# First batch's FFN input layer by halves of the tokens, with its taps in the product's PSUM bank

## The chip, the cores and the metric

One core of a Trainium2 chip. The metric is the device time of one execution in microseconds (us). The kernel before takes 770.74 us (median of 3 runs, 770.47 to 771.9).

## The reference

Three layers follow one another on 4 batches of 576 tokens. Arrays are float32.

```python
scores = scale * q @ k^T                            # 4 x 8 heads x 576 x 576, head width 64
scores = where(scores >= max(scores) - tau, scores, -1e9)
attn   = softmax(scores) @ v                        # heads side by side: x, 4 x 576 x 512
h  = relu(x^T @ w_tok1) @ w_tok2                    # token mixing, 576 -> 256 -> 576
u  = x + h^T
u  = u + relu(u @ w_ch1) @ w_ch2                    # channel mixing, 512 -> 1536 -> 512
h  = relu(u @ w_in)                                 # FFN input layer, 512 -> 1024
c  = w0 * h[s-1] + w1 * h[s] + w2 * h[s+1]          # three taps along the tokens, zero at both ends
out = (h * sigmoid(c)) @ w_out                      # FFN output layer, 1024 -> 512
```

## The kernel before, in words

**Tiling.** A batch has four pairs of heads. Attention works in chunks of 128 queries by 576 keys, nine for a pair, so 36 for a batch. A chunk's chain is: scores into two PSUM banks (`scores`), the row maximum on DVE (`exps`, tile `nm`), the threshold `thr`, the exponential on ACT (tile `e`), the mask on DVE (`mask`, L602), the float16 high half on ACT (`ph`, L607), the low half on POOL (`rest`, L611), one DMA transpose (L616), and the product with V (`pv`, L626 and L629) once the transpose has landed. In the first batch all of a chunk's tiles lie in a ring of four within the buffer `act_t`, so its transposes show as `act_t<-act_t`; later ones as `pt<-ph`. After a pair's nine chunks come the token mixing products (`tok`, L666, L681, L686), which give the transposed activations `u`, high and low half.

**Dense part** (`dense`). Channel mixing takes 12 tiles of w_ch1 (L793) and then 12 of w_ch2 (L811). The FFN input layer follows with 8 tiles `f` of 128 features (L844), and the output layer with five groups of 128 tokens `j` (L867, L870). Each product is three float16 passes. In the FFN input layer a tile's 576 tokens are computed as 256 and 320 columns, each in a PSUM bank that `dbank` hands out and `flush` takes back after the eviction. `h_out` evicts each part with a relu into the float32 tile `h` (L820), which frees the bank. After the second part `gate` works on all 576 tokens in a float32 SBUF tile `ct`: the first tap on ACT (L827), two more on DVE (L829), a tanh on ACT (L831), the product with `h` on DVE (L832), the high half on ACT (L833) and the low half on POOL (L834).

```python
A.activation(out=ct, in_=ht[:, 0:S], func=AF.Copy, scale=cw[:, 0, f:f + 1])
for kk in (1, 2):
    V.scalar_tensor_tensor(out=ct, in0=ht[:, kk:kk + S], scalar=cw[:, kk, f:f + 1], in1=ct, ...)
```

**Interleaving.** The dense part of batch b runs beside the attention of batch b+1: both are generators, advanced in proportion. The weights are loaded and split into halves while the first batch runs (`wload`, `float32`, called by `wstep`), through bank 4, which joins the free banks when the last weight has been asked for. Until then the first batch's dense part has banks 5 and 6.

**Order.** The instructions are first written down in that program order. The class `Order` then puts each engine's instructions in the order in which a list scheduler with fixed costs (`cost`, `send`) would start them, the earliest in program order first among those that are ready. For loads from DRAM there is a further rule, the `heels`: a load that is written down after the fourth and up to the 36th transpose may be placed only when the transpose four places back has been placed. SP issues almost all DMAs in that one order, so an issue that waits holds up those behind it. The 36th transpose is the last of the first batch.

```python
elif self.dma[x] and not self.area(i.ins[0])[9] and self.BEHIND < len(turned) <= self.FIRST:
    self.heels.setdefault(turned[-1 - self.BEHIND], []).append(x)
```

## Time and profile before

| | |
|---|---|
| median of 3 runs | 770.74 us |
| the profiled execution: its time, its span | 770.83 us, 769.0 us |
| busy share: PE, DVE, ACT, POOL | 95%, 66%, 59%, 54% |
| PE idle within the span | 42.2 us (769.0 less 726.8) |
| mean granted TensorE clock | 0.989 |
| chain that ended last: PE, DVE, DMA, POOL, ACT | 67%, 9%, 8%, 5%, 5% |

The share of a busy engine is a mean over stages. Attention of the first batch alone fills the first 97 us; channel mixing of batch 0 beside attention of batch 1 lasts to 226 us; the FFN of batch 0 follows to 300 us. Each further batch takes about 165 us, the last without attention beside it. In the rows below, a line number is that of the kernel before. A row of a group gives its busy time and mean duration, then the idle time of its engine ahead of it and whose end closed that idle time. In a timeline row the idle time ahead stands in brackets with its releaser.

### The profile page before, as it was taken

How to read it: one execution, taken by the hardware profiler on the slowest of the kernel's cores; microseconds unless marked ns; L12 is line 12 of the kernel's file. 1: busy time of each engine (PE TensorE's matmuls, PEld its weight loads, DVE VectorE, ACT ScalarE, POOL GpSimd, SP SyncE). 2: the span in 40 equal slices, each digit the busy share in tenths (PEclk: the TensorE clock that was granted, in tenths of full speed). 3: DMA queues.
4: the chain of work that ended last, by engine and by line, in shares of the span. 5: the costliest groups of instructions: out<-in, count | busy, mean ns of one | idle time of the engine just before them, and what ended most of it. 6: DMA issues, size and time to landing. Idle time of an engine off the chain costs nothing.

```text
span 769.0 us, 18598 instructions
## 1 busy us (share of the span) xinstructions
PE 726.8 (95%) x7398; PEld 543.3 (71%) x7398; DVE 511.2 (66%) x914; ACT 452.8 (59%) x927; POOL 417.8 (54%) x463
## 2 busy tenths in 40 slices
PE   7889769999998879999999999999999999999998
PEld 4567557777776646788888766778888766788764
DVE  6989768887789961676867952776866941323470
ACT  6977757776768842575657752665656842211471
POOL 5877689887878960466555840366464830000040
PEclk9999979999999999999999999999999999999999
DMA  8999999999997702579777502588863400000001
GB/s 215 224 182 177 265 228 211 240 213 229 204 237 170 156 15 83 122 134 158 159 140 135 86 15 93 114 148 148 153 118 63 78 29 35 1 1 2 1 1 62
DMA packets 200951, 97.00 MB, mean 126 GB/s; under 512 B 174752, under 2 KB 186784, under 8 KB 200864
## 3 DMA queue, kind: packets, MB, share of 16 engines
q1 hardware_dynamic: 200544, 95.55, 59.8%
q8 instruction: 58, 0.95, 0.5%
q10 hardware_dynamic: 320, 0.26, 0.1%
q14 instruction: 29, 0.24, 0.1%
HBM read 39.35 MB, written 4.72 MB: 57 GB/s over the span
## 4 chain that ended last, share of the span: by engine, by line
PE 67%; DVE 9%; DMA 8%; POOL 5%; ACT 5%; issue 4%; SPq 2%; ACTq 0%; POOLq 0%; DVEq 0%
PE ps L811 17%; PE ps L793 15%; PE ps L867 11%; PE ps L844 7%; PE ps L571 4%; PE ps L626 3%; DMA act_t<-act_t 3%; DVE ct L829 3%; PE ps L666 2%; PE ps L681 2%; PE ps L567 2%; PE ps L629 2%; DMA ld<-in_v_dram 1%; POOL ph L611 1%; DVE nm L583 1%
## 5 line engine op out<-in xcount | busy, mean ns | idle before, releaser
L611 POOL TENSOR_TENSOR ph<-e,ph 128x576 f16<-128x576 f32 x108 | 141.6, 1311 | 105.7 <-ACT ph L607 93.5
L811 PE MATMUL ps<-act_t,wc_h 128*128 128x256 f16 (+1 forms) x768 | 149.9, 286 | 0.0
L583 DVE TENSOR_REDUCE nm<-ps 128x1 f32<-128x576 f32 x144 | 107.6, 748 | 20.0 <-PE ps L571 12.8
L602 DVE SCALAR_TENSOR_TENSOR e<-ps,thr,e 128x576 f32<-128x576 f32 x108 | 87.6, 812 | 49.4 <-ACT e L595 41.4
L834 POOL TENSOR_TENSOR act_t<-ct,act_t 128x576 f16<-128x576 f32 x32 | 46.0, 1438 | 132.2 <-ACT act_t L833 130.8
L793 PE MATMUL ps<-u_h,wc_h 128*128 128x320 f16 (+1 forms) x384 | 109.6, 286 | 0.5 <-DVE u_l L689 0.5
L811 PE MATMUL ps<-act_t,wc_l 128*128 128x256 f16 (+1 forms) x384 | 109.7, 286 | 0.0
L793 PE MATMUL ps<-u_h,wc_l 128*128 128x320 f16 (+1 forms) x384 | 109.5, 286 | 0.0
L793 PE MATMUL ps<-u_l,wc_h 128*128 128x320 f16 (+1 forms) x384 | 109.1, 286 | 0.0
L793 PEld LDWEIGHTS <-wc_h 128*128 128x128 f16 x768 | 75.1, 98 | 21.5 <-issue 2.1
L811 PEld LDWEIGHTS <-wc_h 128*128 128x128 f16 x768 | 75.1, 98 | 21.0 <-issue 2.0
L867 PE MATMUL ps<-wo_h,act_t 128*128 128x512 f16 x256 | 77.3, 383 | 4.2 <-ACT h L820 4.2
L829 DVE SCALAR_TENSOR_TENSOR ct<-h,cw,ct 128x576 f32<-128x576 f32 x64 | 71.8, 1125 | 7.5 <-ACT ct L827 7.2
L844 PE MATMUL ps<-u_h,wi_h 128*128 128x256 f16 (+1 forms) x256 | 73.0, 286 | 3.5 <-ACT h L820 1.9
L607 ACT ACTIVATE ph<-e 128x576 f16<-128x576 f32 x108 | 73.1, 677 | 1.2 <-DVE e L602 0.8
L844 PE MATMUL ps<-u_h,wi_l 128*128 128x256 f16 (+1 forms) x256 | 73.1, 286 | 0.0
L844 PE MATMUL ps<-u_l,wi_h 128*128 128x256 f16 (+1 forms) x256 | 73.1, 286 | 0.0
L768 DVE SCALAR_TENSOR_TENSOR act_t<-ps,act_t 128x256 f16<-128x256 f32 x96 | 43.5, 455 | 43.2 <-ACT act_t L767 42.6
L867 PEld LDWEIGHTS <-act_t 128*128 128x128 f16 x384 | 36.9, 98 | 47.2 <-issue 6.4
L626 PE MATMUL ps<-vh,pt 128*128 128x65 f16 (+1 forms) x1080 | 68.8, 195 | 0.6 <-DVE x L646 0.6
L626 PEld LDWEIGHTS <-pt 128*128 128x128 f16 (+1 forms) x1080 | 61.2, 101 | 8.8 <-issue 5.7
L767 ACT ACTIVATE act_t<-ps 128x256 f16<-128x256 f32 x96 | 39.1, 407 | 47.9 <-PE ps L793 47.1
(123 smaller groups left out, 1670.5 us busy)
## 6 DMA issues: line engine op xcount, KB each, us to landing
st<-in_moe_w_ch_dram SPq DMA_DIRECT2D x24, 512.0 KB, 4.6
ld<-in_v_dram SPq DMA_DIRECT2D x32, 160.0 KB, 3.1
kt<-ks SPq DMA_DIRECT2D x32, 144.0 KB, 2.8
st<-in_moe_w_in_dram SPq DMA_DIRECT2D x8, 512.0 KB, 5.0
st<-in_moe_w_out_dram SPq DMA_DIRECT2D x8, 512.0 KB, 4.4
out_dram<-ot SPq DMA_DIRECT2D x16, 256.0 KB, 2.0
kt<-in_k_dram SPq DMA_DIRECT2D x16, 144.0 KB, 4.1
ld<-in_q_dram SPq DMA_DIRECT2D x8, 288.0 KB, 3.6
```

The lines of the kernel that those rows point to most:

```text
L583: V.tensor_reduce(out=nm, in_=c["s3"], axis=AX.XY, op=ALU.max, negate=True)
L602: V.scalar_tensor_tensor(out=e3, in0=c["s3"], scalar=c["thr"], in1=e3, op0=ALU.is_ge, op1=ALU.mult)
L607: A.activation(out=c["ph"][:, 0:S], in_=c["e"], func=AF.Copy)
L611: G.tensor_tensor(out=c["ph"][:, S:], in0=c["e"], in1=c["ph"][:, 0:S], op=ALU.subtract)
L626: T.matmul(dst[o:o + m], pt[:, j, o:o + m], vh[:, hh, j, 0:D + 1], start=(j == 0), stop=(j == NSL - 1))
L768: V.scalar_tensor_tensor(out=r_t(f, 1)[:, sl], in0=t, scalar=0.0, in1=r_t(f, 0)[:, sl], op0=ALU.max, op1=ALU.subtract)
L793: T.matmul(t, wc1[wx][:, f, c], u[c][ux][:, sl], start=(c == 0 and i == 0), stop=(c == NC - 1 and i == 2))
L811: T.matmul(t, wc2[wx][:, c, f], r_t(f, rx)[:, sl], start=(by_dve(c) and f == 0 and i == 0), stop=(f == NF - 1 and i == 2))
L829: V.scalar_tensor_tensor(out=ct, in0=ht[:, kk:kk + S], scalar=cw[:, kk, f:f + 1], in1=ct, op0=ALU.mult, op1=ALU.add)
L834: G.tensor_tensor(out=g_t(f, 1), in0=ct, in1=g_t(f, 0), op=ALU.subtract)
L844: T.matmul(t, wi[wx][:, f, c], u[c][ux][:, s0:s0 + n], start=(c == 0 and i == 0), stop=(c == NC - 1 and i == 2))
L867: T.matmul(t, g_t(f, gx)[:, j * P:(j + 1) * P], wo[wx][:, f], **lim)
```

## The change

Three edits. **First**, in the first batch the FFN input layer goes by halves of the tokens: all 8 tiles for the first half, then all 8 for the second. A half has 290 columns, the 288 tokens and one neighbour on each side (at the ends of the sequence the column is the zero margin or falls on the far side). `h_half` does the relu into one of four half-size slots in the two `h` tiles, writes the first tap back over the product in its PSUM bank, adds the two other taps there, applies the tanh there, and writes the product with `h` to an SBUF tile `ct`; only then is the bank free. `wstep` is called with 1 at each of the 16 halves instead of 2 at each of the 8 tiles. Batches 1 to 3 keep the form of before. **Second**, the `heels` rule: loads that are written down after the 31st to 36th transpose wait for the 36th to be placed. **Third**, in batches 0 and 1 (72 chunks) `thr` moves from DVE to ACT.

```diff
--- before.py
+++ after.py
@@ -33,12 +33,14 @@
         self.dma = [i.opcode in ("DMACopy", "DmaTransposeAnt") for i in self.ins]
         self.before, self.first, self.uses, self.turns = [set() for _ in range(n)], [[] for _ in range(n)], [[] for _ in range(n)], {}
         self.depend()
-        self.heels, turned = {}, []
+        self.heels, turned = {}, 0
+        turns = [x for x, i in enumerate(self.ins) if i.opcode == "DmaTransposeAnt"]
         for x, i in enumerate(self.ins):
             if i.opcode == "DmaTransposeAnt":
-                turned.append(x)
-            elif self.dma[x] and not self.area(i.ins[0])[9] and self.BEHIND < len(turned) <= self.FIRST:
-                self.heels.setdefault(turned[-1 - self.BEHIND], []).append(x)
+                turned += 1
+            elif self.dma[x] and not self.area(i.ins[0])[9] and self.BEHIND < turned <= self.FIRST:
+                heel = turned - 1 - self.BEHIND if turned <= self.LAST else self.FIRST - 1
+                self.heels.setdefault(turns[heel], []).append(x)
         self.after = [[] for _ in range(n)]
         for x in range(n):
             for y in self.before[x]:
@@ -143,7 +145,7 @@
         size = o[7] * o[8] * o[6]
         return size / (390 if size > 2e5 else 300), 500, 1450, 1250 if s[9] and o[9] else 1750 if o[9] else 1300
 
-    BEHIND, FIRST = 3, 36
+    BEHIND, LAST, FIRST = 3, 30, 36
     LAP = {"DVE": 85, "Activation": 103, "Pool": 44}
     LAG = {"DVE": 24, "Activation": 24, "Pool": 76, "SP": 17, "PE": 30}
 
@@ -437,10 +439,11 @@
 
     u_t = [[[const.tile([P, S], F16, name=f"u{i}_{c}_{x}") for x in "hl"] for c in range(NC)]
            for i in range(2)]
-    h_t = [const.tile([P, S + 2], F32, name=f"h{i}") for i in range(2)]
+    HW = S // 2 + 4
+    h_t = [const.tile([P, 2 * HW], F32, name=f"h{i}") for i in range(2)]
     for t in h_t:
-        V.memset(t[:, 0:1], 0.0)
-        V.memset(t[:, S + 1:S + 2], 0.0)
+        for o in (0, HW - 1, HW, 2 * HW - 1):
+            V.memset(t[:, o:o + 1], 0.0)
     v_t = [(const.tile([P, 2, 2 * NS + 1, D + 2], F16, name=f"vh{i}"),
             const.tile([P, 2, NS + 1, D], F16, name=f"vl{i}")) for i in range(2)]
     qk_t = [(const.tile([P, 2, S], F16, name=f"qt{i}"),
@@ -590,7 +593,7 @@
         if kind:
             G.tensor_scalar(out=thr, in0=nm, scalar1=-1.0, scalar2=mtaus[:, 1:2], op0=ALU.mult, op1=ALU.add)
         else:
-            V.tensor_scalar(out=thr, in0=nm, scalar1=-1.0, scalar2=mtaus[:, 0:1], op0=ALU.mult, op1=ALU.add)
+            A.activation(out=thr, in_=nm, func=AF.Identity, scale=-1.0, bias=mtaus[:, 0:1])
         e = half(i, 0).bitcast(F32) if i < PER else qk2.tile([P, S], F32, tag="x", name="e", bufs=15)
         A.activation(out=e.rearrange("p (a b) -> p a b", a=2), in_=c["s3"], func=AF.Exp, bias=bias,
                                    scale=sc)
@@ -833,9 +836,40 @@
             A.activation(out=g_t(f, 0), in_=ct, func=AF.Copy)
             G.tensor_tensor(out=g_t(f, 1), in0=ct, in1=g_t(f, 0), op=ALU.subtract)
 
-        for f in range(NG):
-            if b == 0:
-                wstep(2)
+        def h_half(f, x, t):
+
+            ht = h_t[f % 2][:, (f // 2 + x) % 2 * HW:][:, :HW]
+            A.activation(out=ht[:, 1:HW - 1], in_=t, func=AF.Relu, scale=1.0 / WS2)
+            ct = t[:, :hn]
+            A.activation(out=ct, in_=ht[:, 2 * x:2 * x + hn], func=AF.Copy, scale=cw[:, 0, f:f + 1])
+            for kk in (1, 2):
+                V.scalar_tensor_tensor(out=ct, in0=ht[:, 2 * x + kk:2 * x + kk + hn], scalar=cw[:, kk, f:f + 1], in1=ct,
+                                       op0=ALU.mult, op1=ALU.add)
+            A.activation(out=ct, in_=ct, func=AF.Tanh, scale=0.5 / SX)
+            gt = qk2.tile([P, S], F32, tag="x", name="ct", bufs=15)[:, :hn]
+            V.scalar_tensor_tensor(out=gt, in0=ct, scalar=1.0, in1=ht[:, 2 * x + 1:2 * x + 1 + hn], op0=ALU.add, op1=ALU.mult)
+            gh, gl = [g_t(f, y)[:, x * hn:(x + 1) * hn] for y in range(2)]
+            A.activation(out=gh, in_=gt, func=AF.Copy)
+            G.tensor_tensor(out=gl, in0=gt, in1=gh, op=ALU.subtract)
+
+        if b == 0:
+            for x in range(2):
+                for f in range(NG):
+                    wstep(1)
+                    bk = dbank()
+                    s0 = x * (hn - 2)
+                    t = ps[:, bk, :hn + 2]
+                    for c in range(NC):
+                        for i, (wx, ux) in enumerate(PASS):
+                            T.matmul(t, wi[wx][:, f, c], u[c][ux][:, s0:s0 + hn + 2],
+                                     start=(c == 0 and i == 0), stop=(c == NC - 1 and i == 2))
+                    flush()
+                    late.append((bk, lambda f=f, x=x, t=t: h_half(f, x, t)))
+                    yield
+            flush()
+            for t in h_t:
+                V.memset(t[:, S + 1:S + 2], 0.0)
+        for f in range(NG if b else 0):
             for s0, n in SPL:
                 bk = dbank()
                 t = ps[:, bk, :n]
```

How the order moves. On SP, around the last ten transposes of the first batch. Before (`st` are weights, `ld` is V, `qt` and `kt` are Q and K of the next batch):

```order
L347 DMA st<-in_moe_w_ch_dram 128x1024 x3
L616 DMA_TRANSPOSE act_t<-act_t 128x9x128 x4
L347 DMA st<-in_moe_w_ch_dram 128x1024
L513 DMA ld<-in_v_dram 128x320 x2
L616 DMA_TRANSPOSE act_t<-act_t 128x9x128 x4
L347 DMA st<-in_moe_w_ch_dram 128x1024
L473 DMA qt_166<-in_q_dram 128x576
L482 DMA kt_0_167<-in_q_dram 64x576
L616 DMA_TRANSPOSE act_t<-act_t 128x9x128
L528 DMA vh_159<-vh_159 64x2x264
```

And now, the same place:

```order
L349 DMA st<-in_moe_w_ch_dram 128x1024 x3
L619 DMA_TRANSPOSE act_t<-act_t 128x9x128 x9
L349 DMA st<-in_moe_w_ch_dram 128x1024
L516 DMA ld<-in_v_dram 128x320 x2
L349 DMA st<-in_moe_w_ch_dram 128x1024
L476 DMA qt_170<-in_q_dram 128x576
L485 DMA kt_0_171<-in_q_dram 64x576
L486 DMA kt_1_172<-in_k_dram 64x2x288
```

Six loads that stood among the last nine transposes now stand behind them.

On DVE, in the FFN input layer of the first batch. Before (L829 are the taps, L832 the product, L593 is `thr`, L583 the maximum, L602 the mask):

```order
L593 TENSOR_SCALAR thr<-nm,mtaus 128x1
L829 SCALAR_TENSOR_TENSOR ct<-h_154,cw,ct 128x576
L583 TENSOR_REDUCE nm<-ps 128x1
L829 SCALAR_TENSOR_TENSOR ct<-h_154,cw,ct 128x576
L593 TENSOR_SCALAR thr<-nm,mtaus 128x1
L602 SCALAR_TENSOR_TENSOR e<-ps,thr,e 128x576 x2
L832 SCALAR_TENSOR_TENSOR ct<-ct,h_154 128x576
```

And now (L846 are the taps, L850 the product, L388 and L390 convert weights, L586 and L605 are the maximum and the mask):

```order
L586 TENSOR_REDUCE nm<-ps 128x1
L846 SCALAR_TENSOR_TENSOR ps<-h_154,cw,ps 128x288 x2
L388 SCALAR_TENSOR_TENSOR ps<-st,ps 128x512
L850 SCALAR_TENSOR_TENSOR ct<-ps,h_154 128x288
L390 SCALAR_TENSOR_TENSOR wf<-st,ps 128x512
L605 SCALAR_TENSOR_TENSOR e<-ps,thr,e 128x576
L846 SCALAR_TENSOR_TENSOR ps<-h_153,cw,ps 128x288 x2
L586 TENSOR_REDUCE nm<-ps 128x1
```

Three instructions of 576 columns with SBUF operands have become six of 288 columns, each with one operand in PSUM; `thr` is gone.

On ACT, in the same stage, now (L842 is the relu, L844 the first tap, L848 the tanh, L852 the high half, L596 `thr`; L598, L610, L375 and L387 are the exponential, the chunk's high half and two steps of a weight):

```order
L848 ACTIVATE ps<-ps 128x288
L842 ACTIVATE h_154<-ps 128x290
L375 ACTIVATE wo_h<-wf 128x512
L852 ACTIVATE act_t<-ct 128x288
L844 ACTIVATE ps<-h_154,cw 128x288
L596 ACTIVATE thr<-nm,mtaus 128x1
L387 ACTIVATE ps<-st 128x512
L842 ACTIVATE h_153<-ps 128x290
L848 ACTIVATE ps<-ps 128x288
L598 ACTIVATE e<-ps,nm 128x576
```

The steps of two halves alternate, one in bank 5 and one in bank 6, with attention and weights between them. In the built program all 16 halves lie in these two banks in turn, a token mixing product of 30 matmuls takes bank 6 once between two halves, and bank 4 is first used behind the twelfth half, for a token mixing product and then for the output layer. On PE 16 matmuls of the output layer stand between the last four halves; after the last half come 14 matmuls of the output layer, 7 of `pv`, 18 of the output layer, 30 of token mixing and then the other 96 of the output layer. Before, all the output layer's matmuls stood behind the last tile of the input layer: 48, with 12 token mixing and 56 `pv` matmuls among them, then the 30 and the 96. From that point on the order of every engine is the same in both kernels.

## Rows read from the trace of the kernel before

**Rows 1.** Windows: stretch, length, busy PE, PEld, DVE, ACT, POOL, granted clock, DMA share, GB/s.
```profile
0.00:97.00 97.00, 78.63 (x846) 55.43 (x846) 82.00 (x190) 74.79 (x141) 71.17 (x82) 0.98 1.02 212
97.00:114.66 17.66, 11.69 (x154) 8.97 (x151) 10.46 (x24) 9.46 (x19) 14.67 (x19) 0.71 1.12 237
114.66:226.00 111.34, 109.95 (x1129) 82.18 (x1128) 90.42 (x181) 80.30 (x156) 92.76 (x103) 1.00 1.01 223
226.00:289.30 63.30, 54.00 (x565) 38.02 (x564) 56.00 (x80) 44.42 (x87) 51.02 (x45) 0.97 0.54 117
```

**Rows 2.** Lines, 226 to 289 us: busy time, mean ns | idle ahead and its releaser.
```profile
L829 DVE SCALAR_TENSOR_TENSOR ct<-h,cw,ct 128x576 f32<-128x576 f32 x16 | 22.2, 1393 | 0.0
L832 DVE SCALAR_TENSOR_TENSOR ct<-ct,h 128x576 f32<-128x576 f32 x8 | 8.9, 1117 | 0.8 <-ACT ct L831 0.8
```

**Rows 3.** Tile view of ct, 226 to 290 us: minimum, median, maximum in ns.
```profile
L829 DVE SCALAR_TENSOR_TENSOR ct<-h,cw,ct x16: 805/1584/1826, 232.8 to 280.0; 128x576 f32<-128x576 f32 x16
```

**Rows 4.** Lines by form over the whole run (columns as rows 2).
```profile
L602 DVE SCALAR_TENSOR_TENSOR e<-ps,thr,e 128x576 f32<-128x576 f32 x108 | 87.6, 812 | 49.4 <-ACT e L595 41.4 <-POOL thr L591 6.5 <-DMA pt<-ph 0.6
L775 DVE SCALAR_TENSOR_TENSOR us<-ps,u_h 128x256 f32<-128x256 f32 x9 | 3.8, 417 | 6.7 <-PE ps L811 6.7
L386 DVE SCALAR_TENSOR_TENSOR ps<-st,ps 128x512 int32<-128x512 int32 x42 | 28.9, 689 | 7.4 <-ACT ps L385 4.1 <-issue 1.6 <-POOL st L382 1.4
L593 DVE TENSOR_SCALAR thr<-nm,mtaus 128x1 f32<-128x1 f32 x72 | 14.6, 204 | 0.4
L588 ACT ACTIVATE bias<-nm 128x1 f32<-128x1 f32 x72 | 14.4, 201 | 45.4 <-DVE nm L583 45.0
```

**Rows 5.** Timeline of PE: start, duration, what; then chain of waits to 300 us.
```profile
273.03 1.01 PE L867 MATMUL ps<-wo_h,act_t 128*128 128x512 f16 x2 [4.18 <-ACT h L820]
...
229.61 4.68 PE ps L844 x36
...
287.67 1.68 PE ps L666 x30
...
289.34 10.37 PE ps L867 x48
```

**Rows 6.** Timeline of the SP queue: start, duration of issue, what.
```profile
86.99 0.90 SPq L513 DMA_DIRECT2D ld<-in_v_dram  x2
...
97.03 2.23 SPq L616 DMA_TRANSPOSE act_t<-act_t  x1
...
103.50 0.62 SPq L529 DMA_DIRECT2D vh<-vh  x1
```

**Rows 7.** Chain of waits to 119 us, then timelines of PE and POOL.
```profile
97.03 6.74 DMA act_t<-act_t
...
106.99 3.31 PE ps L666 x30
...
114.66 4.25 PE ps L793 x36
...
103.81 0.24 PE L626 MATMUL ps<-vh,act_t 128*128 128x65 f16 x1 [4.93 <-DMA act_t<-act_t]
...
95.01 1.28 POOL L611 TENSOR_TENSOR act_t<-act_t 128x576 f16<-128x576 f32 x1 [0.44 <-PE ps L629]
```

**Rows 8.** DMA view: tile, queue, issues, size, median us to landing.
```profile
vh<-vh SPq DMA_DIRECT2D x32, 66.0 KB, 3.2
act_t<-act_t SPq DMA_TRANSPOSE x36, 3.7
```

**Rows 9.** Two short windows (columns as rows 1).
```profile
103.80:107.00 3.20, 2.20 (x23) 1.18 (x24) 2.01 (x5) 0.73 (x2) 1.53 (x3) 0.50 1.04 266
...
273.00:276.00 3.00, 2.97 (x8) 1.08 (x8) 2.95 (x5) 2.75 (x6) 3.00 (x3) 0.54 0.00 0
```

**Rows 10.** Timelines of ACT and DVE: first tile of the FFN input layer.
```profile
231.49 0.44 ACT L820 ACTIVATE h<-ps 128x320 f32<-128x320 f32 x1 [0.23 <-PE ps L844]
...
236.72 1.68 DVE L832 SCALAR_TENSOR_TENSOR ct<-ct,h 128x576 f32<-128x576 f32 x1
```

## The prediction

> **What bounds the kernel now.** I read the windows by stage first. The reader is to see which engine is full in each [rows 1]. In channel mixing, 114.66 to 226 us, PE works 109.95 of 111.34 us, so nothing that another engine saves there shows. Two stretches are not bound by PE. From 97 to 114.66 us PE is idle for 17.66 − 11.69 = 5.97 us and its mean granted clock is 0.71. From 226 to 289.3 us, the FFN input layer, PE works 54.0 of 63.3 us (9.3 idle) and DVE is the fullest engine with 56.0. Then I read, inside these two, the chain of waits, the queue of SP and the groups of lines. Before 97 us the chains of the chunks decide; the change touches only `thr` there. Behind the token mixing product of 30 matmuls and the 96 output matmuls, whose first 48 start at 289.34 [rows 5], every engine has the same order in both kernels, so that part keeps its length and starts earlier or later.
>
> **Base.** The profiled execution took 770.83 us, a span of 769.0 and 1.83 around it; the median of the runs is 0.09 less, which I neglect.
>
> **Late loads.** Before, SP issued the 36th transpose at 97.03 [rows 6], although POOL had finished its data at 95.01 + 1.28 = 96.29 [rows 7]: loads stood ahead of it. Without them it goes 0.74 earlier. It landed 6.74 us after its issue [rows 7], against a median of 3.7 for the 36 [rows 8]; with no loads sharing the DMA engines I take the median, 3.04 less. PE waited 4.93 us for it [rows 7] and would wait 1.2. Third, after that idle time PE ran at a granted clock of 0.50, the level of 1.2 GHz [rows 9]; its 30 token mixing matmuls took 3.31 us [rows 7], where the same 30 took 1.68 later [rows 5]: 1.63. With a wait of 1.2 us I expect no fall. Sum: −0.74 − 3.04 − 1.63 = **−5.4**. Bounds: 0, if the landing is slow for another reason, and −9.5, all the idle 5.97 and about 3.5 for all that ran at half clock. I take the middle value, since each piece has its own row.
>
> What now stands behind the transposes is six loads: two pieces of V for the next batch's first pair, Q, K and two weights. The weights have slack, I take 0 for them. V goes on from the load through POOL and ACT to two shifts on SP, and is priced below as a rival.
>
> **`thr` on ACT.** In the first 97 us DVE loses 36 × 0.204 = 7.3 of 82.0 us, and ACT gains 36 × 0.201 (its one-column step) = 7.2 on 74.8 [rows 1, 4]. Neither is full and a chunk's chain passes through both, so I take 0. Bounds: half of what moves, ±3.6. The other 36 lie in stages that PE bounds, or count below.
>
> **FFN input layer by halves.** The 16 taps and 8 products of before took 22.2 + 8.9 = 31.1 us of DVE [rows 2]. They become 48 instructions of 288 columns with one operand in PSUM. No row shows one; the nearest are L602 (a PSUM operand, 576 columns, 812 ns) and L775 (256 columns, 417 ns) [rows 4]: 395 ns for 320 columns, so 417 + 32 × 1.234 = 456 ns for 288. A PSUM destination does not look dearer: L386, with one, took 689 ns for 512 columns [rows 4]. So 48 × 0.456 = 21.9, and DVE has 56.0 − 31.1 + 21.9 − 6 × 0.2 (`thr`) = 45.6. The upper bound is half of the old mean, 0.70, and a little more fixed cost: 0.74, with which DVE would have 59.2.
>
> Why 0.456 rather than 0.74: the same SBUF tap took 805 ns at its fastest and 1584 in the median [rows 3], while POOL was busy for 51 of the 63 us; L602, which reads PSUM, stays at 812 in the mean, POOL busy or not. The Trainium skill, page "SBUF — State Buffer", section "Who interferes with whom", says that a DVE instruction with two SBUF inputs contends with GpSimd reads, and one with at most one SBUF input does not. By that rule the estimate is the 0.456 above; if it failed for the taps it would be the upper bound, a rival below. The trace agrees so far as SBUF taps and L602 go.
>
> ACT gets 24 instructions more, at no more than 0.2 fixed cost each, and six `thr`: at most 44.4 + 6 = 50.4. POOL stays near 51 [rows 1]. PE needs 54.0 less the half clock after its longest wait, 2.97 × (1 − 0.54) = 1.4 [rows 5, 9], so 52.6, and would be the fullest. The columns of the product barely grow (16 × 290 for 8 × 576). So the stage can gain 0 to 63.3 − 52.6 = 10.7. I let half of the old idle time stay, 4.65: 57.2, **−6.1**.
>
> A check by turns of a bank, since a bank is now held until the product with `h`. There are 8 turns on each of banks 6 and 5. A half is 12 matmuls at 4.68/36 = 0.13 [rows 5], 1.5 us; then relu, first tap, tanh at 0.44 [rows 10] and three DVE steps at 0.456: 4.2, about 4.4 with the steps' gaps. Call the turn t. The big output group would start at 226 + 1.5 + 7t + 3 (the 30 token mixing matmuls take one turn of bank 6) + 12.5 (what stands behind the last product: 42 output matmuls at 10.37/48 = 0.216, a half, and the 30) = 243 + 7t. For 57.2 t must be 5.75. Unqueued it is 4.4. In the old form relu to product of the first tile took 238.40 − 231.49 = 6.9 [rows 10], where its steps alone need about 4.6 (relu 0.44, two ACT steps at twice that, three DVE steps at 0.805 [rows 3]); with that queueing, 2.3, t is 6.7. 5.75 lies between, and DVE is less full, 45.6 of 57.2 against 56.0 of 63.3. The stage is no gain from t = 6.6.
>
> Sum: 770.8 − 5.4 + 0 − 6.1 = **759.3 us**.
>
> **Rivals.**
> *V comes late* (15%). The load of V is issued behind the 36th transpose, at 96.29 + 2.23 = 98.5. Before, it took 103.50 − 86.99 = 16.5 us from that issue to the second shift [rows 6], and a shift lands in 3.2 [rows 8]: 118.2. PE now wants it later in its order, behind the 36 matmuls of the first channel mixing tiles: the 30 token mixing matmuls ended at 110.30 and would end at 104.9; add 4.36 for what stood between that and 114.66 (28 `pv` matmuls among it, neglected), and 4.25 [rows 7]: 113.5. PE would wait 4.7, most of the early gain: 764.0. Against it: 7 of the 16.5 us were four transposes ahead in the queue, which now stand before V. Without them it lands about when it is wanted.
>
> *The taps stay dear* (5%): 0.74 each, DVE 59.2 of 63.3, the stage gains nothing: 765.4.
>
> *The banks turn too slowly* (12%, the slower side). Only two banks serve all halves, and each is held through six steps on two shared engines. If these queue in all eight turns as for the old first tile, t = 1.5 + 6.9 = 8.4, the group starts at 243 + 58.8 = 301.8, 12.5 late: 770.8 + 12.5 − 5.4 = 777.9. The point from which the whole is slower than before is 243 + 7t = 289.3 + 5.4, t = 7.4. Against it: 6.9 holds three DVE steps at up to 1.68 [rows 10], not 0.46.
>
> *The clock falls at the hand-offs* (4%). PE waits in each turn; if each wait cost what the one at 273 us did, 1.4, eight cost 11.2: 57.2 + 11.2 = 68.4, 770.8 + 5.1 − 5.4 = 770.5. The Trainium skill, page "TensorE: Matmul & The Clock Gate", section "A second HAM failure mode: psum-queue depth-cycling", tells of such a kernel, whose clock went up and down as PE idled briefly between groups. Against it here: the stage held a mean of 0.97 with 9.3 us idle [rows 1].
>
> *Better than that* (8%): early loss wholly gone, −9.5, and the stage near PE's need: below 754.
>
> **Numbers.** My forecast, 754 to 764, has 56%. The range 752 to 767 takes in the forecast, late V, dear taps and most of the better case; the slower case and the clock case stay out. A measurement of this kernel can tell about 0.2%, 1.5 us, from no change. Faster: 56 + 15 + 5 + 8 = 84%; the same, the clock case: 4%; slower: 12%.
>
> **What the profile after would show.** Right: the last transpose of the first batch lands within about 4 us, PE waits under 2 us for it, and its clock stays near 1.0 in the next token mixing product; the tap and product lines show about 0.46 each; DVE has about 46 in the stage and PE's idle time there is 5 or less, its clock 1.0; the big output group starts near 278, 11.5 earlier. Wrong: PE waits for the shift of V near 114 us; taps at 0.7; PE's idle time in the input layer goes to the last DVE product of a bank, with turns above 6.6 us; or the granted clock falls within the stage.

## The result and the profile after

The changed kernel took 776.76 us (median of 5 runs) where the kernel before took 770.74: a ratio of 1.0075, interval 1.0053 to 1.0096. The forecast was 759.3, range 752 to 767. The profiled execution took 775.81 us, a span of 773.9.

The windows by stage, with the columns of [rows 1], first the four stretches of before and then the input layer alone, from its first matmul to the 48 output matmuls that stand in one row:

```profile
0.00:97.00 97.00, 78.50 (x828) 55.32 (x829) 74.63 (x149) 76.77 (x169) 68.78 (x77) 0.96 0.99 201
97.00:114.66 17.66, 13.34 (x163) 9.58 (x162) 11.91 (x25) 12.75 (x28) 13.90 (x19) 1.00 1.08 245
114.66:226.00 111.34, 110.61 (x1143) 82.24 (x1141) 90.14 (x159) 86.23 (x183) 95.87 (x106) 1.00 1.01 229
226.00:289.30 63.30, 50.88 (x514) 35.20 (x512) 47.63 (x99) 47.78 (x115) 41.85 (x52) 0.95 0.59 119
...
225.09:293.99 68.90, 56.48 (x565) 38.98 (x564) 48.54 (x101) 49.36 (x118) 43.63 (x54) 0.95 0.57 117
```

In the kernel before that stage ran from 225.96 to 289.34, 63.38 us, PE busy for 54.08 at a clock of 0.97. Now it starts 0.9 earlier and ends 4.65 later: 68.90 us, PE idle for 68.90 − 56.48 = 12.4. DVE fell from 56.0 to 48.5 and is no longer the fullest engine, and yet PE waits more. Behind it nothing changed: from the 48 matmuls to the end of the span 479.7 before and 479.9 after.

What PE waited for in that stage (what waited, on which engine's result: us, times, longest):

```profile
PE ps L629 <- DMA pt<-ph: 6.4, 4, 3.5
PE ps L864 <- DVE ct L850: 3.6, 4, 1.3
PE ps L864 <- DVE rl L675: 0.9, 1, 0.9
```

The taps and the product on DVE in that stage, and `thr` on ACT over the run (lines view, columns as [rows 2, 4]):

```profile
L846 DVE SCALAR_TENSOR_TENSOR ps<-h,cw,ps 128x288 f32<-128x288 f32 x32 | 16.6, 518 | 6.4 <-ACT ps L844 6.0
L850 DVE SCALAR_TENSOR_TENSOR ct<-ps,h 128x288 f32<-128x288 f32 x16 | 7.2, 453 | 1.7 <-ACT ps L848 1.6
...
L596 ACT ACTIVATE thr<-nm,mtaus 128x1 f32<-128x1 f32 x72 | 20.7, 288 | 12.3 <-DVE nm L586 12.1
```

The price of a tap was 0.518 us and of the product 0.453, against 0.456 in the forecast; `thr` costs 0.288 on ACT, not 0.201. PE waits 3.6 us for banks, and 6.4 for transposed chunks, 3.53 of it at 239.45. The granted clock behind that wait, and in the stretch with the waits for banks after it (windows, columns as [rows 1]):

```profile
238.00:246.00 8.00, 6.55 (x40) 3.99 (x41) 3.16 (x7) 3.06 (x8) 5.11 (x6) 0.57 0.78 203
246.00:262.00 16.00, 11.26 (x121) 7.68 (x119) 14.93 (x31) 15.57 (x39) 13.33 (x17) 1.00 0.61 116
```

The chain of waits shows what stood ahead of the transpose that came late:

```profile
232.06 1.16 POOL wi_l L376
233.22 1.24 POOL ph L614
234.49 4.91 DMA pt<-ph
...
240.39 2.90 PE ps L864 x12
```

PE's timeline shows it and the first waits for a bank:

```profile
239.45 0.24 PE L629 MATMUL ps<-vh,pt 128*128 128x65 f16 x1 [3.53 <-DMA pt<-ph]
...
247.82 0.28 PE L864 MATMUL ps<-u_h,wi_h 128*128 128x290 f16 x1 [1.29 <-DVE ct L850]
...
252.01 0.28 PE L864 MATMUL ps<-u_h,wi_h 128*128 128x290 f16 x1 [1.33 <-DVE ct L850]
```

A weight step and then the chunk's low half hold POOL from 232.06, the transpose goes out at 234.49 and PE, which works in order, stands at 235.9. 12 input layer matmuls then take 2.90 us in place of some 1.5.

The early part as windows: the first 90 us, from there to the end of the 30 token mixing matmuls, and on to the first `w_ch2` matmul, which has the same PE work ahead of it in both. First the kernel before, then the changed one:

```profile
0.00:90.00 90.00, 73.32 (x772) 51.59 (x772) 75.80 (x177) 68.55 (x128) 64.86 (x74) 0.98 1.01 211
90.00:110.30 20.30, 12.64 (x170) 9.52 (x170) 13.76 (x32) 12.61 (x24) 17.08 (x21) 0.79 1.14 223
110.30:160.62 50.32, 50.32 (x469) 37.05 (x469) 42.81 (x85) 38.42 (x78) 44.92 (x52) 0.98 0.99 221
```

```profile
0.00:90.00 90.00, 71.50 (x730) 49.58 (x731) 70.80 (x142) 72.64 (x160) 62.88 (x73) 0.97 0.99 205
90.00:105.32 15.32, 13.50 (x205) 10.61 (x203) 10.87 (x23) 11.35 (x26) 12.46 (x14) 0.94 0.99 217
105.32:160.72 55.40, 52.17 (x477) 37.68 (x478) 44.33 (x80) 43.00 (x95) 49.58 (x58) 1.00 1.02 223
```

PE's idle time in the three stretches (length less busy time) was 16.7, 7.7 and 0 us, and is now 18.5, 1.8 and 3.2. The change wins 5.8 in the middle and loses 1.8 ahead of it and 3.2 behind it; the same work also keeps PE busy for 0.9 longer, so `w_ch2` begins at 160.7, where it began at 160.6. The same place on PE's timeline and on ACT's:

```profile
103.18 0.44 PE L669 MATMUL ps<-xh,wt_h 128*128 128x128 f16 x5 [0.43 <-ACT xh L657]
...
112.71 0.30 PE L796 MATMUL ps<-u_h,wc_h 128*128 128x320 f16 x1 [1.85 <-DVE u_l L692]
```

```profile
111.03 0.77 ACT L493 ACTIVATE kt<-kt,qsc 128x576 f32<-128x576 f32 x1 [1.90 <-DMA kt<-in_k_dram]
111.71 0.42 ACT L691 ACTIVATE u_h<-ps 128x320 f16<-128x320 f32 x1
```

PE does not wait for the 36th transpose any more, and its 30 token mixing matmuls begin at 103.18 at full clock. But K of the next pair, issued at 102.89, lands after 8.06 us (chain of waits). ACT waits 1.90 for it to scale it, the eviction `u_h` is queued behind that on ACT, and PE waits 1.85 for `u_l`. K itself is not among the six loads that moved: the load into `kt` that did move reads `in_q_dram`, so it is a second piece of Q. In the kernel before this piece of K was issued at 102.21, also behind the 36th transpose, and landed after 4.12 us. What is new is that all six moved loads now stand ahead of it. That alone does not make up the delay: with the same loads moved this piece landed after 6.40 in e1 below, and after 8.57 in e4, which has `thr` on ACT as well.

### The profile page after: what moved, and what is told of

Read it like the earlier page. It is cut to its first block, busy times and chain, and to the rows that moved or that the text cites. A ratio compares the mean times of both kernels' runs of the same rounds, so it can differ in the third digit from the quotient of the medians.

```text
span 773.9 us, 18609 instructions
## 1 busy us (share of the span) xinstructions
PE 730.6 (94%) x7398; PEld 544.1 (70%) x7398; DVE 496.9 (64%) x872; ACT 468.5 (61%) x1023; POOL 409.5 (53%) x471
## 4 chain that ended last, share of the span: by engine, by line
PE 67%; DMA 11%; ACT 6%; POOL 6%; DVE 5%; issue 3%; SPq 1%; POOLq 0%; ACTq 0%; DVEq 0%
PE ps L814 18%; PE ps L796 12%; PE ps L901 11%; PE ps L878 6%; PE ps L629 4%; DMA act_t<-act_t 3%; PE ps L574 3%; PE ps L570 3%; PE ps L669 2%; POOL ph L614 2%; PE ps L684 2%; PE ps L632 2%; DMA pt<-ph 2%; PE ps L864 2%; DMA kt<-in_k_dram 2%
## 5 line engine op out<-in xcount | busy, mean ns | idle before, releaser
L586 DVE TENSOR_REDUCE nm<-ps 128x1 f32<-128x576 f32 x144 | 107.4, 749 | 24.9 <-PE ps L574 12.5
L605 DVE SCALAR_TENSOR_TENSOR e<-ps,thr,e 128x576 f32<-128x576 f32 x108 | 87.7, 813 | 51.9 <-ACT e L598 43.6
L837 POOL TENSOR_TENSOR act_t<-ct,act_t 128x576 f16<-128x576 f32 x24 | 34.4, 1432 | 128.4 <-ACT act_t L836 127.0
L610 ACT ACTIVATE ph<-e 128x576 f16<-128x576 f32 x108 | 73.2, 677 | 1.0 <-DVE e L605 0.8
L878 PE MATMUL ps<-u_h,wi_h 128*128 128x256 f16 (+1 forms) x192 | 54.9, 286 | 1.3 <-ACT h L823 1.0
L878 PE MATMUL ps<-u_h,wi_l 128*128 128x256 f16 (+1 forms) x192 | 54.9, 286 | 0.0
L878 PE MATMUL ps<-u_l,wi_h 128*128 128x256 f16 (+1 forms) x192 | 54.9, 286 | 0.0
L832 DVE SCALAR_TENSOR_TENSOR ct<-h,cw,ct 128x576 f32<-128x576 f32 x48 | 49.7, 1038 | 7.5 <-ACT ct L830 7.1
```

The lines of the kernel that those rows point to most:

```text
L586: V.tensor_reduce(out=nm, in_=c["s3"], axis=AX.XY, op=ALU.max, negate=True)
L605: V.scalar_tensor_tensor(out=e3, in0=c["s3"], scalar=c["thr"], in1=e3, op0=ALU.is_ge, op1=ALU.mult)
L610: A.activation(out=c["ph"][:, 0:S], in_=c["e"], func=AF.Copy)
L878: T.matmul(t, wi[wx][:, f, c], u[c][ux][:, s0:s0 + n], start=(c == 0 and i == 0), stop=(c == NC - 1 and i == 2))
```

## The experiments

Points in time of each profiled execution (us): the first `w_ch2` matmul, the first input layer matmul, the 48 output matmuls (the later row of 48 where token mixing splits them), the stage between the last two, and the ratio of the whole to the kernel before. PE's work up to the first `w_ch2` matmul and up to the first input layer matmul is the same in the built order of before, of the changed kernel and of the kernels with one or two of its three edits. Each ratio is to runs of the kernel before that were taken beside it; from e1 on their medians are 768.7 to 769.6 us. e8 to e14 are one execution each and leave out or lighten weights, so they have no ratio and stand below the table.

| kernel | w_ch2 | input layer | 48 | stage | ratio (interval) |
|---|---|---|---|---|---|
| before | 160.6 | 226.0 | 289.3 | 63.4 | 1 |
| changed | 160.7 | 225.1 | 294.0 | 68.9 | 1.0075 (1.0053 to 1.0096) |
| late loads alone (e1) | 158.8 | 223.4 | 292.5 | 69.0 | 1.0052 (1.0033 to 1.0071) |
| `thr` alone (e2) | 164.8 | 228.5 | 291.1 | 62.6 | 1.0045 (1.0026 to 1.0064) |
| halves alone (e3) | 160.5 | 224.2 | 293.0 | 68.8 | 1.0070 (1.0047 to 1.0094) |
| late loads and `thr` (e4) | 162.0 | 226.4 | 291.2 | 64.8 | 1.0016 (0.9993 to 1.0039) |
| changed, taps in SBUF (e5) | 158.6 | 223.0 | 293.2 | 70.2 | 1.0097 (1.0079 to 1.0115) |
| late weights (e6) | 159.4 | 223.8 | 293.2 | 69.5 | 1.0074 (1.0058 to 1.0090) |
| changed, third bank (e7) | 160.7 | 226.9 | 296.6 | 69.7 | 1.0135 (1.0085 to 1.0185) |
| `thr` in batch 1 (e15) | 162.1 | 226.9 | 290.0 | 63.1 | 1.0021 (1.0010 to 1.0032) |
| pace (e16) | 159.6 | 223.5 | 290.8 | 67.3 | 1.0024 (1.0010 to 1.0038) |
| last three loads (e17) | 157.2 | 221.6 | 290.5 | 69.0 | 1.0035 (1.0020 to 1.0050) |
| late Q, K, V (e18) | 164.1 | 228.2 | 296.4 | 68.2 | 1.0102 (1.0074 to 1.0130) |

### One edit at a time

e1 to e4 are the kernel before with one or two of the three edits of the diff above.

> The kernel before with the late loads alone. Theory A (the loads moved behind the transposes come back as a wait on ACT: K of the next pair lands late and its scaling step holds the relu and copies queued behind it): the 30 token mixing matmuls start some 4 us earlier as in the changed kernel, but PE waits near 111 us and most of it is lost by the first channel mixing of w_ch2; the whole is 0 to 2 us faster than before (769 to 771). Rival (the loads were right and `thr` on ACT took the gain): 765 to 766, the forecast's 5.4 less.

> The kernel before with `thr` on ACT alone. Theory A: within 1 us of before, since neither ACT nor DVE is full in the first 97 us. Rival (`thr` on ACT took the early gain): 2 to 5 us slower, with the loss in the first 115 us and in the rows of ACT.

> The kernel before with the input layer by halves alone. Theory B (two banks held for some 4.4 us each turn set the stage): the stage from the first input layer matmul to the 96 output matmuls is 68 to 70 us against 63.3, the whole 775 to 777. Rival (the halves are good, and it is the one wait of 3.5 us for a transposed chunk with the half clock behind it, an accident of the order of the changed kernel, that costs): no such wait here, the stage is at most 63, the whole 768 to 771.

> The changed kernel with the old input layer (late loads and `thr` on ACT kept). Theory A and B: as e1_heels, 769 to 771, which leaves all of the loss to the halves. Rival (`thr` on ACT costs beside the late loads): 2 us or more above e1_heels.

Not one edit is a gain, and they don't add up: 0.52, 0.45 and 0.70% alone, 0.75% together. In e1 the 30 token mixing matmuls ended at 105.6 in place of 110.3, as foretold, but w_ch2 began only 1.8 earlier and the input layer 2.5. So the early gain is 2.5, not 5.4. The part of theory A on the stage ahead held; its total did not, since the old input layer became 5.6 us longer.

e2 went as its rival said in size and place, and theory A missed. It is 0.45% slower; its 36th transpose went out at 101.64 in place of 97.03, the product of the last chunk of the first batch came at 107.8 against 103.8, and w_ch2 began 4.1 later. POOL had finished the data of that transpose at 99.99 in place of 96.29, so most of the loss lies in the chains of the chunks ahead of it. That it lies in ACT's rows, as the rival had it, was not shown. With the late loads as well (e4) that product came at 100.7, only 0.3 later than in e1, but w_ch2 began 3.2 later than in e1: up to there PE was busy for 2.4 us longer with the same work, and idle for 0.8 more. So `thr` on ACT costs 3 to 4 us ahead of w_ch2 in both pairs. How much of it is the step and how much the order that the scheduler finds with it was not taken apart; in e15 below, which moves no step of the first batch, POOL had these data 2.6 later than in the kernel before, and w_ch2 began 1.5 later. In the stage behind, the kernels with `thr` on ACT were shorter, 0.8 in e2 and 4.2 in e4. So e4 missed both its theories: it lies 0.36% below e1, and the halves, the one edit that it lacks, make up some 0.6 of the 0.75% that the changed kernel loses.

e3 showed theory B's size: 68.8 us of stage, with waits for banks of 5.9 and for transposes of 3.5. Its rival was not put to the test, since a wait of 3.2 for a transposed chunk came here too (at 243.74). And one wait for a bank was followed by half clock, on PE's timeline and as a window:

```profile
254.07 0.28 PE L862 MATMUL ps<-u_h,wi_h 128*128 128x290 f16 x1 [2.43 <-DVE ct L848]
```

```profile
254.00:258.00 4.00, 3.93 (x19) 2.54 (x19) 2.91 (x8) 3.57 (x8) 3.80 (x6) 0.57 0.69 177
```

### Which limit the halves have

e5 writes the taps into an SBUF tile and so frees the bank after the relu:

```diff
-            ct = t[:, :hn]
+            ct = qk2.tile([P, S], F32, tag="x", name="ct", bufs=15)[:, :hn]
...
-            gt = qk2.tile([P, S], F32, tag="x", name="ct", bufs=15)[:, :hn]
+            gt = ct
```

> The changed kernel with the first tap, the taps, the tanh and the product with `h` in an SBUF tile: a bank is free after the relu. Theory B (a bank held through six steps sets the stage): PE no longer waits for the product, the stage is 3 us or more shorter than the 66.6 of the changed kernel, the whole 770 to 774, although each tap costs more. Rival (the price of the steps on DVE sets it): with taps that contend for SBUF, 0.7 or more each, the stage is no shorter, 777 or more.

The stage, 70.2 (the changed kernel has 68.9 by the points of the table, not the 66.6 that the expectation names), was as the rival said, and the whole, 776.1, near its 777. PE did stop waiting for the product, as theory B said, but that did not make the stage shorter. Its window:

```profile
223.00:293.20 70.20, 58.16 (x565) 40.11 (x564) 61.70 (x100) 49.23 (x118) 47.83 (x53) 0.93 0.46 112
```

The source view of the taps (minimum, median and maximum in ns), in e5 and then in the changed kernel:

```profile
L846 DVE SCALAR_TENSOR_TENSOR ct<-h,cw,ct x32: 500/780/1622, 226.9 to 285.8; 128x288 f32<-128x288 f32 x32
```

```profile
L846 DVE SCALAR_TENSOR_TENSOR ps<-h,cw,ps x32: 507/521/524, 228.9 to 286.8; 128x288 f32<-128x288 f32 x32
```

The same tap of 288 columns has a minimum of 500 ns in SBUF and a median of 780, a maximum of 1622; in PSUM it lay between 507 and 524. DVE is busy for 61.7 of 70.2. The forecast's reading of the price, and the Trainium skill's rule (page "SBUF — State Buffer", section "Who interferes with whom") that a DVE instruction with at most one SBUF input does not contend with GpSimd, agree with this. So either place of the taps has its own limit.

To see the form without the load of its surroundings, e8 and e9 leave w_out out, on the changed kernel and on the kernel before (bank 4 joins the free banks behind the input layer there); e13 is e8 with e5's edit:

```diff
-  (w_ch2, wc2, 512, UP2), (w_in, wi, 512, UP2), (w_out, wo, 512, UP2)):
+  (w_ch2, wc2, 512, UP2), (w_in, wi, 512, UP2)):
...
+            for t in wo:
+                G.memset(t.rearrange("p a b -> p (a b)"), 0.01)
```

> The changed kernel without loading and converting w_out (a constant stands in its place), so that no weight is converted in the first batch's input layer; the halves keep banks 5 and 6 alone. Theory B (the bank turns set the stage): with the steps of a half unqueued PE still waits for the product of a half, the stage is 58 to 62 us. Rival (the conversion of w_out in the same queues, with loads that land late, sets it): the waits go, the stage is 53 to 56 us.

> The kernel before without loading and converting w_out, for comparison with e8_no_wout. Theory B: the old form needs less, 54 to 57 us, less than the halves without w_out. Rival (halves are the better form where the queues are free): above the stage of e8_no_wout.

> The halves without w_out (e8_no_wout) and with taps, tanh and product in SBUF, so that a bank is free after the relu. Theory B (the bank held for six steps): the stage (first input layer matmul to the 48 output matmuls in a row) is 54 to 58 us, against some 63 in e8_no_wout, although DVE is busier. Rival (many short steps through two engines, or their price on DVE): 61 or more.

The stage as a window, in e8, in e9 and in e13:

```profile
229.36:291.99 62.63, 53.54 (x565) 37.87 (x564) 39.36 (x85) 41.66 (x103) 29.67 (x38) 1.00 0.32 61
```

```profile
232.18:285.12 52.94, 51.37 (x557) 37.10 (x556) 39.95 (x62) 35.51 (x69) 32.79 (x28) 1.00 0.35 66
```

```profile
228.59:288.09 59.50, 54.44 (x565) 39.59 (x564) 46.72 (x84) 40.69 (x103) 32.38 (x38) 0.97 0.34 64
```

And PE's longest wait in e8's stage:

```profile
PE ps L862 <- DVE ct L848: 5.0, 5, 1.8
```

With no weight of w_out in the queues the old form needs 52.9 us, PE idle for 1.6. The halves need 62.6, PE idle for 9.1, with no engine above two thirds but PE: DVE is as busy as in the old form. PE waits above all for the product that frees a bank. Freed after the relu (e13) PE is idle for 5.1, though DVE works 7 us more. So of the 7.5 us of idle time more, 4.0 go when the bank is freed after the relu; the rest was not taken apart. e8 and e9 came out in the order that theory B said, 0.6 above its range and 1.1 below it; e13's 59.5 lies between the two bounds that were set.

Two runs with a third bank settled nothing. e7 converts the weights in SBUF to free bank 4; e10 adds bank 4 to e8's halves.

> The changed kernel with a third bank for the halves: from the input layer on, the weights are converted in SBUF, which frees bank 4. Theory B: with three banks a turn may take half as long again before PE waits for it; PE's waits for the product of a half fall from 3.6 us to under 1, the stage is 3 us or more shorter than 68.9 (from the first input layer matmul to the 48 output matmuls in one row), the whole 769 to 773, though each of 18 conversion steps on DVE costs more. Rival (the two banks are not what sets it, or the dearer conversions eat the gain): 68 or more, 775 or more.

> The halves without w_out (e8_no_wout) and with bank 4 as a third bank, so that nothing becomes dearer. Theory B: the stage falls from some 62 to the 53 to 55 of the old form without w_out (e9_no_wout_before), with no wait of PE for a half's product. Rival (the longer way of a half through ACT and DVE, three engine changes for each of 16 halves, costs whatever the number of banks): 58 or more.

In e7 the 18 conversion steps grew to a mean of 1195 and 1061 ns, from 692 and 679, and DVE was busy for 55.5 us of the stage, from 48.5. PE's waits for the product of a half did not fall, as theory B had it, but rose to 9.4 us, and the rival's bounds held. In e10 the stage was 70.0, 7.4 longer than in e8: PE's waits for the product fell from 5.3 to 2.4 us, but PE waited 7.6 for the conversion of w_in, whose weights still pass through bank 4 and queued behind the halves there. So e10's total doesn't tell the theories apart.

### Why the late loads lose what they win

e6, e17 and e18 move the loads of one kind: weights; only those behind the 35th transpose (a weight and two pieces of Q); Q, K and V. e11 and e12 are before and e1 with a quarter of the bytes for the last third of w_ch1 and for w_ch2. The edit of e6, against the rule of e1:

```diff
-                heel = turned - 1 - self.BEHIND if turned <= self.LAST else self.FIRST - 1
+                heel = turned - 1 - self.BEHIND if turned <= self.LAST or "_w_" not in self.area(i.ins[0])[0] else self.FIRST - 1
```

(In e18 it stands without the `not`; e17 has e1's rule with LAST 34.)

> The kernel before with the late rule for weights alone; Q, K and V keep their places. Theory A (a K load that lands late holds ACT): no wait of PE behind ACT's scaling of K near 111 us; the first w_ch2 matmul starts 2 us or more before the kernel before's, unless the 36th transpose is as late as there. Rival (any load that is moved behind the transposes is missed later, since the DMA engines are busy for the whole of the first 226 us): w_ch2 starts no earlier than in the kernel before, and the weights of the input layer's stage come later, as in e1_heels.

> The kernel before with a quarter of the bytes for the last third of w_ch1 and for w_ch2 (the quarter is used four times), so that the DMA engines are not busy all the time after the first batch's attention; the conversions stay. For comparison with e12_light_late. Both theories: the first w_ch2 matmul comes at 158 to 161 us, since PE bounds this part.

> The late loads of e1_heels, with those lighter weights. Theory A' (the late loads pay since the DMA engines are full until 226 us, so what is moved behind the transposes lands late, K above all): with free DMA engines K lands in 5 us or less, and the 4 to 5 us that are won at the 30 token mixing matmuls are still there at the first w_ch2 matmul: 4 us or more before e11_light. Rival (the order on SP or the queue of ACT loses them, whatever the DMA engines carry): 2 us or less before e11_light.

> The kernel before with the late rule for loads behind the 35th transpose alone: three loads move from ahead of the 36th transpose to behind it, V and the other weights keep their places. Theory C (weights converted later, within the stage): the input layer starts 2 us or more earlier, one weight is hardly later, the stage is 63 to 65 us: 767 to 769, 0 to 2 below the kernel before. Rival (an earlier start of the stage is given back whatever moved): the stage grows by what was won, 769 to 772.

> The kernel before with the late rule for Q, K and V alone; the weights keep their places. Theory C: nine weights are converted in the stage as in the kernel before, the stage is 63 to 65 us, and the early gain of about 2 us stays: 767 to 769. Rival: 69 us of stage as in e1_heels, 771 to 773.

Theory C missed in e17 and e18, and of the theories on e6 neither held whole. In e6, with K kept in its place, one piece of K landed late again (6.1 us), w_ch2 began 1.2 earlier (theory A had 2, its rival 0) and the stage took 69.5. In e17 the stage gave back the 4.4 us that were won ahead of it and 1.2 more, as its rival said. In e18 the stage of 68.2 was the rival's, but nothing was won ahead of it: w_ch2 began 3.5 later, and the whole, 778.0, is above both ranges.

e11 and e12 were to take the DMA engines' load out as a cause, but lighten it too late for that: their DMA share was 0.56 and 0.67 between 125 and 160 us, while in e12 from 97 to 110 us, where K is issued and lands, it stayed at 1.03 to 1.12, and K landed after 7.2 and 6.9 us. e12's token mixing matmuls ended 4.2 us before e11's, w_ch2 began 2.0 and the input layer 2.5 earlier: as in e1 without the lighter weights. So a lighter load behind 125 us gave nothing back; what the load ahead of it costs stays open. Some of the 4 us never was a gain: in before, 28 `pv` and four score matmuls stood ahead of the first channel mixing product which in e1 stand behind it. They had covered the waits between the token mixing steps: from the first of the 30 token mixing matmuls to channel mixing PE had no idle time in before, and 1.8 us in e1.

Then the stage. e17 began it 4.4 us earlier, and ended it 1.2 later. The last low half of w_out on POOL's timeline, in the kernel before, in e1 and in e17:

```profile
278.22 1.67 POOL L374 TENSOR_TENSOR wo_l<-wf,wo_h 128x512 f16<-128x512 f32 x1
```

```profile
282.83 1.44 POOL L376 TENSOR_TENSOR wo_l<-wf,wo_h 128x512 f16<-128x512 f32 x1 [0.20 <-ACT wo_h L375]
```

```profile
280.89 1.44 POOL L376 TENSOR_TENSOR wo_l<-wf,wo_h 128x512 f16<-128x512 f32 x1 [0.20 <-ACT wo_h L375]
```

The 48 output matmuls began 9.4, 8.2 and 8.2 us behind it. e1 converts ten weights in the stage, before nine. But no wait of PE there is for a weight. Its longest waits in e1's stage, and the stage as a window:

```profile
PE ps L846 <- ACT h L822: 9.2, 2, 5.3
PE ps L869 <- ACT h L822: 1.1, 1, 1.1
```

```profile
223.43:292.45 69.02, 56.54 (x565) 39.22 (x564) 55.92 (x84) 45.93 (x90) 53.99 (x48) 0.93 0.53 116
```

PE waits for the relu `h`, which frees a bank and is queued on ACT behind other steps. In before the waits for it were 5.1 us in all, 4.18 the longest. PE's idle time grew from 9.3 to 12.5 us and its busy time, with a granted clock of 0.93 in place of 0.97, from 54.1 to 56.5. If the conversion of w_out in the same queues is the cause, the loss must go with w_out. e14 is e1 without it:

> The late loads with the old input layer, without w_out. Theory C (the late loads push the conversion of weights into the input layer's stage): without w_out the stage is as short as in e9_no_wout_before, 53 to 54 us, and the gain ahead of it stays. Rival (the late loads disturb the attention of the second batch itself): the stage is 3 us or more longer than in e9_no_wout_before.

```profile
224.92:278.59 53.67, 52.13 (x560) 37.03 (x559) 42.98 (x67) 37.58 (x74) 37.46 (x32) 1.00 0.38 78
```

Its stage as a window is 53.7 against 52.9 in e9. So theory C holds for the stage where it was put to the test: without w_out the late loads do not make it longer. That the gain ahead of it stays was not shown. e14 took 759.8 us and e9 766.9 (one execution each), but e9's early part is itself late (its 36th transpose was issued at 103.96, w_ch2 began at 168.2), and e14 began w_ch2 at 160.7, as the kernel before did, and the input layer at 224.9, 1.0 earlier than it. Which loads are late matters less than theory A and C had it: e18 moved no weight and lost all the same. It too converts ten weights in the stage, the last of w_out done at 288.2.

### Two attempts at a faster version

```diff
-                        wstep(1)
+                        wstep(1 + (f == 0))
```

(e16, in the w_ch2 products, where bank 4 may also join the free banks only once; e15 guards the new `thr` with `if i < PER` for the old one.)

> The kernel before with `thr` on ACT in the second batch alone (the first batch keeps it on DVE). Theory: the first 97 us are as before, the input layer's stage, in which DVE is the fullest, 0.5 to 1.5 us shorter as in e2_thr: 768 to 769.5 where the kernel before takes 769. Rival: the order that the scheduler finds changes more than that, 1 us or more either way.

> The kernel before with four more conversion steps during the w_ch2 products, so that four fewer weights are converted in the input layer's stage. Theory (from e9_no_wout_before: all eight gone make the stage 10 us shorter): the stage is 3 to 5 us shorter, the w_ch2 products, in which DVE and POOL have room, at most 1 longer: 765 to 767. Rival (the loads of the weights are late anyway, or POOL's queue fills in the w_ch2 products): 769 or more.

Both theories missed, and the times were those of the rivals. e15's stage gained 0.3, but the order ahead of it changed and the input layer began 0.9 later. In e16 the last weight of w_out was done 7 us earlier, at 272.5, but nine conversions still fell into the stage, which ended no earlier: its granted clock was 0.92, with waits of PE for a mask (3.3) and for token mixing (2.8). So it is not the last weight alone that ends the stage, and what does there stays open. No version beat the kernel before.

## Why the prediction was wrong

**Late loads, −5.4.** Its three pieces came about as foretold: the 36th transpose went out at 96.68 and landed after 3.21 us, PE did not wait for it, and the token mixing product ended at 105.3, where 104.9 was foretold. The step that failed is the one behind it: that this gain is carried through to the input layer, with "0" for the weights. At w_ch2 nothing of it was left in the changed kernel and 1.8 us in e1; the input layer began 0.9 and 2.5 earlier. Behind the token mixing matmuls PE had no idle time up to w_ch2 before, and now has 3.2 us. In the first 90 us it is idle for 1.8 more; `thr` on ACT goes with that (1.5 more in e2 than before, 1.1 more in e4 than in e1). *V comes late* foresaw a load that lands too late, but not which: it was K, which had not moved and stood behind the loads that had, and it held ACT and through it PE, for 1.85 us.

**`thr`, 0.** The price was 0.288, and ahead of w_ch2 the edit cost 4.1 us alone and 3.2 beside the late loads, at the edge of the bounds of ±3.6. So the 0 failed as well: that neither engine is full did not make the move free. The stage behind gave back 0.8 and 4.2.

**Halves, −6.1.** The sum of DVE's work was near (48.5 against 45.6, and 56.0 before). The step that failed is "I let half of the old idle time stay": 12.4 us of idle time are there in place of 4.65. It took the fullest engine as the bound, with PE at 52.6. But PE works through its order over two banks, and each bank waits for a way of six steps through two queues. e8 shows it with DVE at 39 of 63 us.

The check by turns had the bounds 4.4 and 6.7 and called 5.75 likely. In the changed kernel a bank's turn, from the first matmul of a half to that of the next half in the same bank, took 7.6 us in the mean of the 14 turns: 1.8 for the matmuls, 0.2 up to the relu, 4.3 from there to the end of the product (from 3.2 to 5.6), and 1.3 until PE took the bank again. The last piece, which the check put at nothing, is PE at other work or waiting for a transposed chunk: in 6 of 14 turns PE took the bank within 0.1 us, in the others 0.3 to 4.7 later. *The banks turn too slowly*, with 12%, foretold 8.4 us a turn and 777.9 in all, and the whole came to 776.8. Its mechanism was half of it and its number in part luck: it had 6.9 us from relu to product, where 4.3 were measured, and no late PE. With w_out in the queues, transposed chunks that come late and hold PE cost more (6.4) than the bank itself (3.6).

The clock case came in part. Half clock cost some 56.48 × 0.05 = 2.8 us of the stage (an estimate), before 54.08 × 0.03 = 1.6, and the forecast had left it out. In the changed kernel it followed the wait for a transposed chunk, and the clock was 1.00 through the hand-offs between 246 and 262 us; in e3 it also followed a hand-off, the wait of 2.43 us at 254.07. (The Trainium skill's page "TensorE: Matmul & The Clock Gate", section "A second HAM failure mode: psum-queue depth-cycling", tells of a clock that goes up and down as PE idles briefly between groups. In the changed kernel's trace this is not seen; in e3's it is, once.)

**The sum.** −0.9 for the start and +5.5 for the stage make the 4.65 by which the 48 matmuls came later; the forecast had −5.4 and −6.1. Both terms that were to bring the gain failed, each on waits behind the place where the work was saved.

## What to carry to other kernels

An engine's busy time in a stage is a lower bound, not a forecast: before less work on the fullest engine is called a gain, count the buffers that turn, how long one is held through all the queues on its way, and how soon the engine that fills it comes back to it. A gain ahead of a stage is worth only what the slowest chain in that stage starts earlier: with the conversion of w_out in the queues the stage became 4.8 to 6.1 us longer in e1, e6, e17 and e18, and without it, in e14, it did not. Where a scheduler orders the queues, test each edit alone: here `thr` on ACT, one column for each chunk, moved the last transpose of the first batch from 97.0 to 101.6 us.

## What was unexpected of the hardware

A step on ACT with one column took 0.288 us with a scale and a bias from SBUF, where the one-column step that was used as its price took 0.201. A tap of 288 columns with one operand and its result in PSUM took 0.518, the product, with its result in SBUF, 0.453. That is not the price of a PSUM result: in e5, with all in SBUF, the fastest tap took 0.500 and the fastest product 0.442. No length of a wait parted those that were followed by half clock from those that were not: the granted clock fell to 0.57 behind a wait of 3.53 us in the changed kernel and of 2.43 in e3 (at 254.07), and it stayed at 1.00 behind one of 2.66 in e3 (at 262.43) and the hand-offs of 0.8 to 1.3 in the changed kernel.
